# Block means kept in the value buffers, one token to a partition for keys and queries, PSUM banks given out singly, a shorter weight conversion, and a new plan

## The chip, the cores and the metric

The kernel runs on one core of a Trainium2 chip. The metric is the device time of one execution in microseconds (us). A core has five engines that this text names: TensorE (PE, matrix products; its weight loads are shown apart as PEld), VectorE (DVE), ScalarE (ACT), GpSimd (POOL) and SyncE (SP, which here only issues DMAs). They run their own instruction queues in order and wait for one another through semaphores. PE writes its results into eight PSUM banks.

## The reference

Three layers run one after the other on 1536 tokens (2 batches of 768): attention with 8 heads of 64, a gated layer, and a layer with an ELU. The weights arrive as 64-bit floats, q, k and v as 32-bit floats.

```python
# attention: block = 32, window = 16
k_sum = k.reshape(B, H, nb, block, D).max(axis=3)      # 24 block maxima of the keys
v_sum = v.reshape(B, H, nb, block, D).mean(axis=3)     # 24 block means of the values
scores_l = scale * q @ k^T, kept where |i - j| < 16
scores_s = scale * q @ k_sum^T + log(block)
a = softmax(concat(scores_l, scores_s))
x = a @ concat(v, v_sum)
# gated layer
xn = x / sqrt(mean(x * x) + 1e-6) * rms_g
x = (silu(xn @ w_gate) * (xn @ w_val)) @ w_out          # 512 -> 1536 -> 512
# ELU layer
h = x @ w_in                                            # 512 -> 2048
out = where(h > 0, h, exp(min(h, 0)) - 1) @ w_out2      # -> 512
```

## The kernel before

**Attention** goes in 24 tiles of 64 queries (12 for each batch), all heads at once. A tile needs 96 local keys and values (its own 64 and 16 on each side) and the 24 block maxima and means: 120 columns. The steps of a tile: `copy_keys` (POOL or ACT) builds the key tile `ka` from the transposed keys `kT` and the maxima `ksum`; for the first 8 tiles `premask` puts the mask into PSUM by matmuls; `scores` adds the products, so that mask and scores stand in one bank; `row_max` (DVE), `exps` (ACT), `guard` and `invert` (DVE), `normalize` (POOL for the first 8 tiles, else ACT), `turn_e` (PE transposes), `copy_e` (out of PSUM), `apply_v` (PE), `copy_x`. Since the maxima reach over all 768 keys of a batch, no scores can start until all its keys have been loaded, transposed, copied and reduced.

**Keys, queries, values.** A key load `load_k` brings 256 tokens of four heads, two neighbouring tokens to a partition, so that a run in memory is 512 bytes; the transposes then yield two half tiles that two copies interleave into `kT`. The first 512 queries come in the same way (`load_qq`, `turn_qq`, `copy_qq`), later ones one token to a partition (`load_q`, 256-byte runs). `mean_v` computes the block means by matmuls into PSUM; `copy_v` takes them to SBUF, four DMAs (`place_v`) bring them to a tile `vs`, and one more DMA for each attention tile (`load_vs`) copies `vs` into rows 96 to 119 of that tile's value buffer `va`, of which there are four.

**Weights** pass a chunk of 512 KB at a time through four staging buffers: `fetch` (SP), then the conversion from the 64-bit words: `convert_a` scales the high words as 32-bit floats (ACT), `convert_b` shifts them by three bits and clears the sign bit, `convert_c` puts the sign back, `convert_d` adds the low bits (all DVE). `split_a` and `split_b` turn a chunk into a coarse and a fine part, and three matmuls with these parts stand for one precise product (`project`, `down`).

**Order.** Tokens go through the gated layer in three blocks of 512, then through the ELU layer. A planner, `Order`, holds every step with its engine, a cost in us and a due time, simulates the engines and issues the steps in the order in which they start there; `pool` tags are buffers that a step takes, and a step waits in the plan for a free one. The table `SHIFT` moves due times by the step's name and the stretch of the run. PSUM: two banks under the tag `mm`, two under `at`, and `a0` to `a3`, one each; the tables `EARLY`, `KTAGS`, `QTAGS` and `VTAG` say by hand which tag a step of the first eight tiles takes.

Of the kernel before, what the change touches and what calls it, by code (L numbers as in the profile page):

```python
# [21 lines left out]
P = 128  # L22
BLOCK = 32
# [11 lines left out]
LIGHT = {"mean_v": 0.7, "apply_v": 0.65, "turn_qq": 0.5}  # L35


class Order:
# [34 lines left out]
    def issue(self):  # L73
# [47 lines left out]

        def can(i):
            need = {}
            for tag, name in ops[i][7]:
                need[tag] = need.get(tag, 0) + 1
                if self.slots[tag][1] and name not in queue[tag][:need[tag]]:
                    return False
            return all(free[tag] >= k for tag, k in need.items())
# [4 lines left out]
        while len(started) < n or events:  # L133
            for engine in list(soon):
# [18 lines left out]
                for tag, name in new:  # L153
# [37 lines left out]
def fused_kernel(ctx: ExitStack, tc: tile.TileContext, q, k, v, w_gate, w_val, w_out, rms_g, w_in2, w_out2, out):  # L191
# [45 lines left out]
    pool("va", 4, True)  # L237
# [4 lines left out]
    pool("vs", 1, True)  # L242
# [7 lines left out]
    for tag, bufs in (("mm", 2), ("at", 2), ("a0", 1), ("a1", 1), ("a2", 1), ("a3", 1)):  # L250
        pool(tag, bufs, space=PSUM)
# [34 lines left out]
    ANY_2 = {DVE: 0.6}, {POOL: 1.22, DVE: 0.6}, {POOL: 1.22}  # L286
# [101 lines left out]
    def convert_a(eng, kind, c):  # L388
        hi = words(kind, c).bitcast(F32)
        times(eng, hi, hi, 2.0 ** -112)  # L390

    def convert_b(kind, c):
        hi = words(kind, c)
        t = new("raw", f"raw_{kind}{c}", [P, 512], U32)
        nc.vector.tensor_scalar(
            t, hi, 3, 0x7FFFFFF8, op0=ALU.logical_shift_left, op1=ALU.bitwise_and)
# [74 lines left out]
    def add_k(b, due, gap, tags):  # L471
        add("-", 0.0, due, take, "ksum", f"ksum{b}", [P, NP, NB], w=[f"ksum{b}"], new=[("ksum", f"ksum{b}")])
        for i in range(NG):
            j, g = divmod(i, 2)
            tag = tags[i % len(tags)]
            n = f"{b}_{j}{g}"
            at = due + gap * i
            add("SP", 0.73, at - 4, load_k, b, j, g, w=[f"kr{n}"], new=[("raw", f"kr{n}")])
            add(PE, 0.44, at, turn_k, b, j, g, tag, r=[f"kr{n}"], w=[f"kt{n}"], new=[(tag, f"kt{n}")])
            if g == 0:  # L480
                add("-", 0.0, at - 1, take, "kT", f"kT{b}_{j}", [P, NP, 2 * P], w=[f"kT{b}_{j}"], new=[("kT", f"kT{b}_{j}")])
            for r in range(2):
                add(ANY if b == 0 else {ACT: 0.48}, 0, at + 0.5, copy_k, b, j, g, r,
                    r=[f"kt{n}", f"kT{b}_{j}"] + [f"kT{b}_{j}#{g}0"] * r, w=[f"kT{b}_{j}#{g}{r}"])
            if g:
                add(DVE, 1.15, at + 1, max_k, b, j, r=[f"kT{b}_{j}#{gg}{r}" for gg in range(2) for r in range(2)] + [f"ksum{b}"],
                    w=[f"ksum{b}#{j}"])

    def add_q(b, j, due, tag):
        rq, pt, qb = f"qr{b}_{j}", f"qt{b}_{j}", f"qbd{(b * NG + j) % 2}"  # L490
        add("SP", 1.46, due - 6, load_q, b, j, w=[rq], new=[("t2", rq)])
        add(PE, 0.44, due, turn_q, b, j, tag, r=[rq], w=[pt], new=[(tag, pt)])
        for h in range(2):
            add({ACT: 0.48}, 0, due + 0.5, copy_q, b, j, h, r=[pt], w=[f"{qb}#{h}{r}" for r in range(2)])


    def load_qq(j, g):
        nc.sync.dma_start(
            out=new("t2", f"qq{j}{g}", [P, NP, 2, D]),
            in_=q[0].rearrange("(a g) s d -> g a s d", g=2)[g, :, j * 2 * P:(j + 1) * 2 * P, :].rearrange(  # L500
                "h (p r) d -> p h r d", r=2))

    def turn_qq(j, n, tag):
        pt = new(tag, f"qt0_{2 * j + n}", [P, 2, NP, 64])
        ps = slice(64 * n, 64 * n + 64)
        for g in range(2):
            for pr in range(NP):
                nc.tensor.transpose(
                    pt[:, g, pr, :], T[f"qq{j}{g}"][ps, pr].rearrange("p r d -> p (r d)"), ident[ps, ps])

    def copy_qq(eng, j, g, r):
        src = T[f"qt0_{j}"][64 * r:64 * r + 64, g].rearrange("p a (t c) -> p t a c", t=2)
        dst = qbd[j % 2][64 * g:64 * g + 64, :, :, g].rearrange("p t a (c r) -> p t a c r", r=2)[:, :, :, :, r]
        times(eng, dst, src, scale)

    def add_qq(m, due, load, tag):
        j, n = divmod(m, 2)
        if n == 0:
            for g in range(2):
                add("SP", 0.73, load + 0.1 * g, load_qq, j, g, w=[f"qq{j}{g}"], new=[("t2", f"qq{j}{g}")])  # L520
        pt, qb = f"qt0_{m}", f"qbd{m % 2}"
        add(PE, 0.5, due, turn_qq, j, n, tag, r=[f"qq{j}0", f"qq{j}1"], w=[pt, f"{qb}#00"], new=[(tag, pt)])
        for g in range(2):
            for r in range(2):

                add({ACT: 0.27, DVE: 0.33}, 0, due + 0.5, copy_qq, m, g, r,
                    r=[pt] + [f"{qb}#{g}0"] * r + [f"{qb}#0{r}"] * g, w=[f"{qb}#{g}{r}"])
# [530 lines left out]
```

## Time and profile before

| what | us |
|---|---|
| median of 3 runs (lowest, highest) | 654.74 (654.32, 657.03) |
| the profiled execution | 653.92 |
| its span, first to last instruction | 652.2 |
| PE busy in it | 639.4 (98%) |
| DVE, ACT, POOL busy | 477.2, 374.5, 68.7 |

The profile is one execution; its span is 1.7 us shorter than the time that was measured for it, what lies before its first and behind its last instruction. Busy time is the union of the instructions' durations on an engine. PE's matmuls overlap, so that the distance from one start to the next says more about their price than their length: 12 matmuls of 512 columns take 2.72 us in a full stretch.

### The profile page before, as it was taken

The page shows a single profiled execution, that of the slowest core. Times are in us where ns is not written, and L with a number is a line of the kernel's source. Part 1 is how long each engine was busy: PE and PEld are TensorE (multiplying, and loading weights), DVE is VectorE, ACT ScalarE, POOL GpSimd, SP SyncE. Part 2 cuts the span into 40 slices and gives each one's busy share as a digit, 9 for nine tenths or more (in the row PEclk, how much of TensorE's full clock was granted, in tenths as well). Part 3 has the DMA queues.
Part 4 walks back from the last instruction along what each step waited for, and adds up shares of the span by engine and source line. Part 5 has one row for each costly group of instructions (what it writes and reads, how often), then busy time and mean ns, then how long its engine had stood idle before and what let it go on. Part 6 is the DMA issues. An engine that isn't in the chain of part 4 may idle for free.

```text
span 652.2 us, 9445 instructions
## 1 busy us (share of the span) xinstructions
PE 639.4 (98%) x3440; PEld 528.4 (81%) x3440; DVE 477.2 (73%) x860; ACT 374.5 (57%) x829; POOL 68.7 (11%) x125
## 2 busy tenths in 40 slices
PE   7899999999999999999999999999999999999997
PEld 5788787888888888888888888888888888888886
DVE  6899998998945545599999996555675555755554
ACT  5887888878856655655555555443454444544441
POOL 4731103125200100300000000000000000000000
PEclk9999999999999999999999999999999999999999
DMA  9785995653120400003655520000010000100001
GB/s 255 196 236 163 268 282 162 200 168 88 33 47 3 140 1 2 0 13 119 205 180 163 162 65 1 0 1 1 1 65 0 2 0 1 53 13 2 0 1 64
DMA packets 69917, 54.70 MB, mean 84 GB/s; under 512 B 29168, under 2 KB 64176, under 8 KB 69872
## 3 DMA queue, kind: packets, MB, share of 16 engines
q1 hardware_dynamic: 69872, 54.11, 28.8%
q8 instruction: 27, 0.44, 0.3%
q14 instruction: 18, 0.15, 0.1%
HBM read 49.68 MB, written 3.15 MB: 81 GB/s over the span
## 4 chain that ended last, share of the span: by engine, by line
PE 91%; DVE 3%; DMA 2%; ACT 2%; SPq 1%; issue 1%; POOL 0%; ACTq 0%; POOLq 0%
PE acc L893 35%; PE ph L825 20%; PE pg L825 14%; PE s L617 3%; PE pv L667 2%; PE pv_7c L825 1%; PE pv_9c L825 1%; PE pv_11c L825 1%; PE pv_1c L825 1%; DMA va<-vs 1%; PE pv_10c L825 1%; PE pv_6c L825 1%; PE pv_5c L825 1%; PE pv_8c L825 1%; PE pv_2c L825 1%; PE pv_3c L825 1%
## 5 line engine op out<-in xcount | busy, mean ns | idle before, releaser
L825 PE MATMUL ph<-xb,ws_i 128*128 128x512 f32 x576 | 137.9, 389 | 0.0
L893 PE MATMUL acc<-ws_p,act 128*128 128x512 f32 x576 | 137.7, 389 | 0.0
L825 PEld LDWEIGHTS ph<-xb,ws_i 128*128 128x128 f32 x576 | 108.1, 188 | 22.5
L893 PEld LDWEIGHTS acc<-ws_p,act 128*128 128x128 f32 x576 | 108.1, 188 | 22.4
L893 PE MATMUL acc<-act,ws_o 128*128 128x512 f32 x432 | 106.4, 393 | 0.0
L825 PE MATMUL pg<-x,ws_g 128*128 128x512 f32 (+1 forms) x432 | 106.3, 390 | 0.0
L893 PEld LDWEIGHTS acc<-act,ws_o 128*128 128x128 f32 x432 | 80.2, 188 | 16.6
L825 PEld LDWEIGHTS pg<-x,ws_g 128*128 128x128 f32 x432 | 78.2, 188 | 15.3 <-issue 0.2
L283 DVE TENSOR_TENSOR ws_p<-raw_p,ws_p 128x512 fp32r<-128x512 f32 x48 | 33.1, 690 | 48.8 <-ACT ws_p L272 48.8
L272 ACT CAST ws_p<-raw_p 128x512 fp32r<-128x512 f32 x48 | 29.8, 621 | 63.1 <-PE ph L825 57.3
L272 ACT CAST act<-ex 128x512 fp32r<-128x512 f32 x48 | 29.8, 622 | 55.9 <-DVE ex L873 39.3
L880 DVE TENSOR_TENSOR act<-ex,act 128x512 fp32r<-128x512 f32 x48 | 33.1, 691 | 31.3 <-ACT act L272 30.9
L283 DVE TENSOR_TENSOR ws_i<-raw_i,ws_i 128x512 fp32r<-128x512 f32 x48 | 33.1, 689 | 19.1 <-ACT ws_i L272 19.0
L272 ACT CAST ws_i<-raw_i 128x512 fp32r<-128x512 f32 x48 | 29.7, 619 | 28.5 <-PE ph L825 23.1
L283 DVE TENSOR_TENSOR ws_g<-raw_g,ws_g 128x512 fp32r<-128x512 f32 x35 | 25.6, 732 | 18.4 <-ACT ws_g L272 18.0
L272 ACT CAST ws_o<-raw_o 128x512 fp32r<-128x512 f32 x36 | 22.4, 621 | 26.3 <-PE acc L893 6.3
L272 ACT CAST ws_g<-raw_g 128x512 fp32r<-128x512 f32 x35 | 21.6, 618 | 24.9 <-PE pg L825 13.2
L873 DVE SCALAR_TENSOR_TENSOR ex<-ph,ex 128x512 f32<-128x512 f32 x48 | 33.2, 691 | 1.5
L272 ACT CAST ws_v<-raw_v 128x512 fp32r<-128x512 f32 x35 | 21.7, 619 | 16.7 <-PE pv_1c L825 3.2
L283 DVE TENSOR_TENSOR ws_v<-raw_v,ws_v 128x512 fp32r<-128x512 f32 x35 | 25.0, 714 | 6.0 <-ACT ws_v L272 5.9
L272 ACT CAST act<-th 128x512 fp32r<-128x512 f32 x36 | 22.3, 618 | 11.6 <-PE acc L893 5.8
L865 ACT ACTIVATE ex<-ph 128x512 f32<-128x512 f32 x48 | 28.5, 593 | 0.0
(209 smaller groups left out, 987.6 us busy)
## 6 DMA issues: line engine op xcount, KB each, us to landing
st_i<-in_moe_w_in SPq DMA_DIRECT2D x16, 512.0 KB
st_p<-in_moe_w_out SPq DMA_DIRECT2D x16, 512.0 KB
st_g<-in_moe_w_gate SPq DMA_DIRECT2D x12, 512.0 KB
st_v<-in_moe_w_val SPq DMA_DIRECT2D x12, 512.0 KB
st_o<-in_moe_w_out SPq DMA_DIRECT2D x12, 512.0 KB
va<-in_v SPq DMA_DIRECT2D x20, 192.0 KB
kr<-in_k SPq DMA_DIRECT2D x12, 256.0 KB
vtok<-in_v SPq DMA_DIRECT2D x6, 512.0 KB
```

What stands on the lines that cost most here:

```text
L272: nc.scalar.copy(out=out, in_=in_)
L283: (nc.gpsimd if eng == POOL else nc.vector).tensor_sub(out, a, b)
L617: nc.tensor.matmul(pq[:, pr, :], qb[:, t % 2, pr].rearrange("p h c -> p (h c)"), ka[:, pr, :], start=not pre, stop=not pre or pr == NP - 1)
L667: nc.tensor.matmul(pv[64 * h:64 * h + 64, pr, :], va[:, 2 * pr + h, :], at[:, pr, QT * h:QT * h + QT], start=True, stop=True)
L825: nc.tensor.matmul(pt[:, i], wt[:, a, kk * P:(kk + 1) * P], xt[:, c, kk, i], start=(kk == 0 and n == 0), stop=(kk == KM - 1 and n == 2))
L865: nc.scalar.activation(out=new("t2", f"ex{b}_{c}", [P, TB]), in_=T[f"ph{b}_{c}"], func=AF.Exp)
L873: nc.vector.scalar_tensor_tensor(ex, T[f"ph{b}_{c}"], 0.0, ex, op0=ALU.max, op1=ALU.add)
L880: nc.vector.tensor_sub(t[:, 1], T[src], t[:, 0].bitcast(F32))
L893: nc.tensor.matmul(acc, lhsT, rhs, start=(first and n == 0), stop=(last and n == 2))
```

## The change

- The block means stay where they are needed: there are four fixed value buffers `va_bufs` that the tiles use in turn. For the first batch four copies (DVE or ACT) bring the means from PSUM into rows 96 to 119 of buffer 0, for the second batch from the SBUF copy `vm`; `repeat_v` (POOL or ACT) copies them to the other three. `load_vs`, the tile `vs` and its DMAs are gone; a tile loads its 96 values alone.
- Keys and all queries are loaded one token to a partition, in 256-byte runs; a key load covers 128 tokens of all heads, one copy takes its transposes to `kT`, and the maxima are taken by 128 tokens.
- Each PSUM bank has a tag of its own, and a step may name several tags: `pick` takes the first that is free. A new tag `pm` lets at most three mask preloads be open, and a preload waits in the plan for the batch's last maximum.
- For the chunks of `w_gate`, `w_val` and `w_out` (`SIGNED`), the scaling on ACT becomes a parametric ReLU, whose slope for negative values, -2^32, leaves them positive with one exponent bit more, and the shift by three moves that bit into the sign's place. `convert_c` isn't issued for them. `w_in` and `w_out2` keep it.
- Costs, due times and the table `SHIFT` are new (56 entries before, 384 now, of which two stand below).

```diff
@@ Order: a step may name several tags
+        def pick(i):
+            need, found = {}, []
+            for tags, name in ops[i][7]:
+                for tag in tags if isinstance(tags, tuple) else (tags,):
+                    n = need.get(tag, 0) + 1
+                    if free[tag] >= n and (not self.slots[tag][1] or name in queue[tag][:n]):
+                        break
+                else:
+                    return None
+                need[tag] = n
+                found.append((tag, name))
+            return found
...
@@ banks and value buffers
-    for tag, bufs in (("mm", 2), ("at", 2), ("a0", 1), ("a1", 1), ("a2", 1), ("a3", 1)):
-        pool(tag, bufs, space=PSUM)
+    MM, AT, ACC = ("m0", "m1"), ("t0", "t1"), ("a0", "a1", "a2", "a3")
+    BANKS = AT + MM + ACC[::-1]
+    for tag in BANKS:
+        pool(tag, 1, space=PSUM)
+    o.pool("pm", PM)
+    va_bufs = [const.tile([P, H, D], F32, name=f"va{i}") for i in range(VA)]
...
@@ conversion
-        times(eng, hi, hi, 2.0 ** -112)
+        if kind in SIGNED:
+            nc.scalar.activation(out=hi, in_=hi, func=AF.Prelu, scale=2.0 ** -112, alpha=-2.0 ** 32)
+        else:
+            times(eng, hi, hi, 2.0 ** -112)
...
+        if kind in SIGNED:
+            nc.vector.tensor_scalar(t, hi, 3, None, op0=ALU.logical_shift_left)
...
-        add(DVE, 0.6, need - 6.5, convert_c, kind, c, r=[st, raw], w=[raw])
+        if kind not in SIGNED:
+            add(DVE, 0.6, need - 6.5, convert_c, kind, c, r=[st, raw], w=[raw])
...
@@ keys
-    def load_k(b, j, g):
+    def load_k(b, i):
         nc.sync.dma_start(
-            out=new("raw", f"kr{b}_{j}{g}", [P, NP, 2, D]),
-            in_=k[b].rearrange("(a g) s d -> g a s d", g=2)[g, :, j * 2 * P:(j + 1) * 2 * P, :].rearrange(
-                "h (p r) d -> p h r d", r=2))
+            out=new("raw", f"kr{b}_{i}", [P, H, D]),
+            in_=k[b, :, i * P:(i + 1) * P, :].rearrange("h p d -> p h d"))
...
+    def copy_k(eng, b, i):
+        j, r = divmod(i, 2)
+        copy(eng, T[f"kT{b}_{j}"][:, :, r * P:(r + 1) * P], T[f"kt{b}_{i}"])
...
@@ block means
-    def place_v(b):
+    def place_v(eng, b):
+        src = T[f"vm{b}"] if b else T[f"vp{b}"]
         for g in range(4):
-            nc.sync.dma_start(out=T[f"vs{b}"][:, 2 * g:2 * g + 2], in_=T[f"vm{b}"][32 * g:32 * g + NB])
+            copy(eng, va_bufs[0][NL:NK, 2 * g:2 * g + 2], src[32 * g:32 * g + NB])
+
+    def repeat_v(eng, i):
+        if eng == POOL:
+            nc.gpsimd.tensor_scalar(va_bufs[i][NL:NK], va_bufs[0][NL:NK], 1.0, 0.0, op0=ALU.mult, op1=ALU.add)
+        else:
+            copy(eng, va_bufs[i][NL:NK], va_bufs[0][NL:NK])
...
+    def add_place(b, due, gap):
+        add({ACT: 0.72, DVE: 0.6} if b == 0 else {POOL: 1.0}, 0, due, place_v, b, r=[f"vm{b}" if b else f"vp{b}"], w=["va0#s"])
+        for i in range(1, VA):
+            add({POOL: 0.6, ACT: 0.52} if b == 0 else {POOL: 0.6}, 0, due + gap * i, repeat_v, i, r=["va0#s"], w=[f"va{i}#s"])
...
-    def load_vs(b, t):
-        nc.sync.dma_start(out=T[f"va{b}_{t}"][NL:NK], in_=T[f"vs{b}"])
...
@@ tiles
-            add(PE, 0.32, due - 1.5, premask, b, t, tags[1], r=[f"mask_b{mask_of(t)}"], w=[f"s{n}"], new=[(tags[1], f"s{n}")])
+            add(PE, 0.32, due - 1.5, premask, b, t, tags, r=[f"mask_b{mask_of(t)}", f"ksum0#{NG - 1}"],
+                w=[f"s{n}", f"pm{n}"], new=[(tags, f"s{n}"), ("pm", f"pm{n}")])
...
@@ plan
-LOOK, URGENT = 0.2, 20
-A0, A_GAP, LATER = 12.1, 1.275, -1.0
+SIGNED = 'gvo'
+LOOK, URGENT = -0.3, 5
+A0, A_GAP, LATER = 11.8, 1.775, 0.0
...
-TILE8, GAP_1, GAP_2 = 8.0, 10.0, 12.5
+TILE8, GAP_1, GAP_2 = 3.0, 9.4, 10.2
...
+K0, QL, VA, PM = 2.1, (1.4, 5.0, 9.5, 11.5), 4, 3
...
+    ('act_a', 0): -6, ('act_b', 0): -2.5, ('add_mask', 0): 3, ('add_square', 0): 10, ('apply_v', 0): -16.5,
...
-LEN_A, LEN_1, LEN_2 = 8.675, 7.55, 5.35
+LEN_A, LEN_1, LEN_2 = 8.575, 7.55, 6.15
```

How the instructions stand on three engines, before and now. In the names `kr`, `qr` and `qq` are loaded keys and queries, `kt` and `qt` their transposes, `vtok` values for the block means, `vp` the means in PSUM, `s` scores, `at` transposed probabilities, `st_g` a staged weight chunk; a number behind a name counts the tile.

SP's queue from the last key load on, a few rows skipped, before:

```order
L445 DMA kr_21_177<-in_k 128x4x128
L498 DMA qq_218<-in_q 128x4x128
L498 DMA qq_220<-in_q 128x4x128
L530 DMA vtok_0_228<-in_v 128x8x128 x2
L530 DMA vtok_1_229<-in_v 128x8x128
L577 DMA va_0_263<-in_v 80x8x64
L498 DMA qq_329<-in_q 128x4x128
L498 DMA qq_332<-in_q 128x4x128
L577 DMA va_1_278<-in_v 96x8x64
L549 DMA vs_405<-vm_412 24x128 x4
L580 DMA va_0_263<-vs_405 24x512
L580 DMA va_1_278<-vs_405 24x512
```

And now, the same stretch:

```order
L466 DMA kr_5_183<-in_k 128x8x64
L454 DMA qr_0_185<-in_q 128x8x64
L454 DMA qr_1_205<-in_q 128x8x64
L515 DMA vtok_0_229<-in_v 128x8x128 x2
L515 DMA vtok_1_230<-in_v 128x8x128
L454 DMA qr_2_274<-in_q 128x8x64
L575 DMA va_136<-in_v 80x8x64
L454 DMA qr_3_291<-in_q 128x8x64
L575 DMA va_137<-in_v 96x8x64
L575 DMA va_138<-in_v 96x8x64
L575 DMA va_139<-in_v 96x8x64
L395 DMA st_g_462<-in_moe_w_gate 128x4x128
```

The query loads come in singly, two ahead of the values for the means and two between the values of the first tiles; the DMAs of the means (`vs` and `va` from `vs`) are gone.

PE from the last transposes ahead of the first scores on, before (the mask preloads of tiles 4, 5, 6, 1 and 0 stand ahead of these rows):

```order
L609 MATMUL s_2_335<-log_lo,ident_b 128x4x24
L539 MATMUL vp_342<-vtok_0_228,blocks 32x128 x16
L617 MATMUL s_0_314<-ka_0_361,qbd_133 128x120 x4
L617 MATMUL s_1_309<-ka_1_367,qbd_133 128x120 x4
L539 MATMUL vp_342<-vtok_1_229,blocks 32x128 x8
L617 MATMUL s_2_335<-ka_2_381,qbd_134 128x120 x4
L508 MATMUL qt_2_434<-ident,qq_329 128x64 x4
L656 MATMUL at_0_456<-ident,e_0_370 120x128 x4
L617 MATMUL s_3_414<-ka_3_399,qbd_134 128x120 x4
L508 MATMUL qt_3_475<-ident,qq_329 128x64 x4
```

And now, where the first row follows the transposes of the last keys (of a preload only its first matmul is shown):

```order
L462 MATMUL qt_0_293<-ident,qr_0_185 128x128 x4
L602 MATMUL s_0_306<-mask_b_166,ident_b 128x480
L462 MATMUL qt_1_310<-ident,qr_1_205 128x128 x4
L602 MATMUL s_1_318<-mask_b_167,ident_b 128x480
L613 MATMUL s_0_306<-ka_0_302,qbd_140 128x120 x4
L613 MATMUL s_1_318<-ka_1_315,qbd_140 128x120 x4
L524 MATMUL vp_340<-vtok_0_229,blocks 32x128 x8
L602 MATMUL s_2_360<-mask_b_167,ident_b 128x480
L613 MATMUL s_2_360<-ka_2_335,qbd_141 128x120 x4
L524 MATMUL vp_340<-vtok_1_230,blocks 32x128 x8
L652 MATMUL at_0_419<-ident,e_0_324 120x128 x4
```

The first scores now stand behind the transposes of the second query load; four mask preloads and the steps of the block means that stood ahead of them stand behind them, and so does the first transpose of probabilities, as before.

DVE between the first key copy and the first query copy, before (the cast of a mask between them isn't shown):

```order
L274 COPY kT_0_176<-kt_00_196 64x512 x2
L274 COPY kT_1_195<-kt_10_248 64x512
L461 TENSOR_REDUCE ksum_179<-kT_0_176 128x4x8
L274 COPY kT_2_217<-kt_21_273 64x512
L274 COPY kT_2_217<-kt_20_267 64x512
L461 TENSOR_REDUCE ksum_179<-kT_1_195 128x4x8
L461 TENSOR_REDUCE ksum_179<-kT_2_217 128x4x8
```

And now:

```order
L290 COPY kT_0_187<-kt_0_221 128x4x128
L483 TENSOR_REDUCE ksum_203<-kT_0_187 128x4x4 x2
L483 TENSOR_REDUCE ksum_203<-kT_1_204 128x4x4 x2
L483 TENSOR_REDUCE ksum_203<-kT_2_228 128x4x4 x2
L296 TENSOR_SCALAR qbd_140<-qt_0_293 64x8x64
L296 TENSOR_SCALAR qbd_141<-qt_1_310 64x8x64
```

DVE copies one key tile where it copied five half ones (ACT has the other copies), and takes six smaller maxima instead of three.

## Rows read from the trace of the kernel before

**Rows 1.** Windows: stretch; its us, busy per engine (instructions), PEclk, DMA share, GB/s
```profile
0.00:15.00 15.00, 10.29 (x96) 7.68 (x97) 9.99 (x21) 8.28 (x15) 7.20 (x37) 1.00 0.95 256
15.00:41.00 26.00, 23.07 (x284) 20.14 (x285) 21.95 (x55) 21.14 (x85) 16.78 (x30) 1.00 0.90 228
41.00:60.00 19.00, 18.73 (x130) 17.04 (x127) 18.44 (x42) 14.26 (x34) 5.61 (x9) 1.00 0.62 172
60.00:100.00 40.00, 39.02 (x273) 31.07 (x271) 36.53 (x66) 32.99 (x84) 6.11 (x7) 1.00 0.91 249
100.00:300.00 200.00, 200.00 (x1135) 164.39 (x1134) 148.33 (x266) 135.28 (x331) 33.00 (x44) 1.00 0.25 73
300.00:648.00 348.00, 348.00 (x1537) 288.05 (x1535) 241.29 (x413) 162.57 (x284) 0.00 (x0) 1.00 0.15 47
```

**Rows 2.** Timeline of PE, 8 to 45: start, us, instructions [idle before <-releaser]
```profile
10.23 0.70 PE L508 MATMUL qt<-ident,qq 64*128 64x64 f32 x8
10.87 0.38 PE L606 MATMUL s<-mask_b,ident_b 128*128 128x480 bf16 x1
...
11.16 0.37 PE L606 MATMUL s<-mask_b,ident_b 128*128 128x480 bf16 x1
...
14.27 2.05 PE L617 MATMUL s<-ka,qbd 128*128 128x120 f32 x16
16.24 0.65 PE L539 MATMUL vp<-vtok,blocks 128*32 128x128 f32 x16
16.82 1.15 PE L617 MATMUL s<-ka,qbd 128*128 128x120 f32 x8
...
20.04 0.65 PE L656 MATMUL at<-ident,e 128*120 128x128 f32 x4 [1.03 <-POOL e L648]
...
36.93 0.66 PE L439 MATMUL qt<-ident,qr 128*128 128x128 f32 x4
37.42 0.64 PE L656 MATMUL at<-ident,e 128*120 128x128 f32 x4
...
41.22 1.99 PE L836 MATMUL pg<-xT,raw_g 128*128 128x256 f32 x8
```

**Rows 3.** Windows of 2 us with different loads, columns as in rows 1
```profile
2.00:4.00 2.00, 0.07 (x1) 0.10 (x2) 1.70 (x8) 0.06 (x1) 1.67 (x11) 1.00 0.90 268
...
8.00:10.00 2.00, 1.85 (x16) 1.37 (x16) 1.58 (x2) 1.93 (x4) 0.04 (x1) 1.00 1.12 335
18.00:20.00 2.00, 1.01 (x11) 0.74 (x9) 1.67 (x5) 2.00 (x14) 1.86 (x4) 1.00 1.12 181
34.00:36.00 2.00, 2.00 (x20) 2.00 (x19) 2.00 (x6) 2.00 (x5) 0.00 (x0) 1.00 1.22 298
```

**Rows 4.** Timeline of PE's weight loads, the last keys' transposes
```profile
8.78 0.42 PEld L454 LDWEIGHTS kt<-ident,kr 128*128 128x128 f32 x4 [0.35 <-ACT kT L272]
```

**Rows 5.** Timeline of DVE, 8 to 15: last key copies and maxima
```profile
9.47 1.41 DVE L274 COPY kT<-kt 64x512 f32<-64x512 f32 x2 [0.42 <-PE kt L454]
10.80 2.33 DVE L461 TENSOR_REDUCE ksum<-kT 128x32 f32<-128x1024 f32 x2
```

**Rows 6.** Timeline of POOL, 12 to 15: maxima into the first key tile
```profile
13.22 0.28 POOL L585 TENSOR_SCALAR ka<-ksum 128x96 f32<-128x96 f32 x1 [5.17 <-DVE ksum L461]
```

**Rows 7.** Chain of waits, 25 to 50: start, us, what
```profile
27.58 5.07 DMA va<-vs
...
34.66 3.25 DMA va<-vs
...
39.61 0.57 DVE raw_g L400
...
45.30 0.60 DVE raw_v L400
```

**Rows 8.** Groups by shape, 0 to 250: line, tiles, count | busy us, mean ns | idle
```profile
L278 ACT ACTIVATE st_g<-st_g 128x512 f32<-128x512 f32 x12 | 8.2, 685 | 0.4 <-DMA st_g<-in_moe_w_gate 0.4
...
L400 DVE SCALAR_TENSOR_TENSOR raw_g<-st_g,raw_g 128x512 uint32<-128x512 uint32 x12 | 8.2, 686 | 0.0
```

More of the change, by code (lines that the diff above doesn't have):

```diff
@@ L120, in issue @@
                 offer(i)
-        def can(i):
[L123 to L128, printed above, removed]
+        def pick(i):
[10 more added lines that the diff above has]
+            return found
+        def can(i):
+            return pick(i) is not None
         def shared(i, engine):
@@ L152, in issue @@
                     soon[e].remove(best)
-                for tag, name in new:
+                for tag, name in pick(best):
+                    home[name] = self.tag_of[name] = tag
                     free[tag] -= 1
@@ L285, in fused_kernel @@
     ANY = {ACT: 0.48, DVE: 0.6}
-    ANY_2 = {DVE: 0.6}, {POOL: 1.22, DVE: 0.6}, {POOL: 1.22}
+    ANY_2 = {DVE: 0.6}, {POOL: 1.28, DVE: 0.6}, {POOL: 1.28}
     ANY_SB = {ACT: 0.52}
@@ L481, in add_k @@
                 add("-", 0.0, at - 1, take, "kT", f"kT{b}_{j}", [P, NP, 2 * P], w=[f"kT{b}_{j}"], new=[("kT", f"kT{b}_{j}")])
[L482 to L487, printed above, removed]
@@ L489, in add_q @@
-    def add_q(b, j, due, tag):
+            add(ANY if b == 0 else {ACT: 0.48}, 0, at + 0.5, copy_k, b, i, r=[f"kt{n}", f"kT{b}_{j}"], w=[f"kT{b}_{j}#{r}"])
+            add(DVE, 0.6, at + 1, max_k, b, i, r=[f"kT{b}_{j}#{r}", f"ksum{b}"], w=[f"ksum{b}#{i}"])
+    def add_q(b, j, load, due, tag):
         rq, pt, qb = f"qr{b}_{j}", f"qt{b}_{j}", f"qbd{(b * NG + j) % 2}"
-        add("SP", 1.46, due - 6, load_q, b, j, w=[rq], new=[("t2", rq)])
+        add("SP", 1.0, load, load_q, b, j, w=[rq], new=[("t2", rq)])
@@ L492, in add_q @@
         add(PE, 0.44, due, turn_q, b, j, tag, r=[rq], w=[pt], new=[(tag, pt)])
         for h in range(2):
[L494 to L527, printed above, removed]
+            add(ANY if b * NG + j < TPB // 2 else {ACT: 0.48}, 0, due + 0.5, copy_q, b, j, h, r=[pt], w=[f"{qb}#{h}"])
@@ L788, in add_norm @@
             if n >= n_sums:
-                add(POOL, 1.22, due + 0.6 * n, add_square, blk, cs, i, r=[sq], w=[first])
+                add(POOL, 1.28, due + 0.6 * n, add_square, blk, cs, i, r=[sq], w=[first])
         y = f"{blk}{i}"
@@ L896, in add_down @@
         for i, ms in enumerate(groups):
-            add(PE, 0.648 * len(ms), due + 1.3 * i, down, names, ms, act, ws, first, last, feature_major,
+            add(PE, 0.68 * len(ms), due + 1.36 * i, down, names, ms, act, ws, first, last, feature_major,
                 r=[act + "#h", act + "#l", ws + "#h", ws + "#l"], w=[names[m] for m in ms],
@@ new lines @@
+    ('load_q', 2): -8, ('load_v', 2): 2, ('mean_square', 2): -9.5, ('normalize', 2): 4.5, ('place_v', 2): -9,
+    ('premask', 2): 1.5, ('project', 2): -2, ('project_f32', 2): 4.5, ('repeat_v', 2): -4, ('root', 2): -24,
+    ('row_max', 2): -8, ('scale_x', 2): 7, ('scores', 2): -1, ('split_a', 2): -3, ('spread', 2): 4,
+    ('square', 2): 1, ('store', 2): 0.5, ('sum_square', 2): -8.5, ('take', 2): 8, ('turn_e', 2): 0.5,
+    ('turn_k', 2): -8, ('turn_q', 2): 1, ('x_lo', 2): 1.5, ('zero_v', 2): -8, ('act_a', 3): 2,
```

220 lines of the change are left out of this document (138 added, 82 removed), and 4 rows, old and new, of the table EARLY.

## Prediction

> **What bounds the kernel now.** I read the stages first [rows 1]: six stretches, each with TensorE's (PE's) busy time beside its length. From 100 to 648 us PE is busy 548.00 of 548 us, at a granted clock of 1.00 throughout. Nothing done for the other engines there can shorten the run, unless PE itself gets less to do. PE is idle 4.71 us before 15 us, 2.93 from 15 to 41, 0.27 from 41 to 60, 0.98 from 60 to 100, and the last 4 us are the output's copy and store, which the change leaves as they are. So the change is worth what it does to about 9 us of idle time, plus what it does to PE's own work, plus a little that busy time hides.
>
> Next I read PE's own order in the attention of the first 512 tokens [rows 2]. A step's price on PE is the distance from its start to the next one's: a mask preload 0.29 us (10.87 to 11.16), eight query transposes 0.64 (10.23 to 10.87), four transposes of 128 tokens 0.49 (36.93 to 37.42), a block-mean step of 16 matmuls 0.58 (16.24 to 16.82), one tile's scores 0.98 (two in 14.27 to 16.24). The first scores start at 14.27 and the first projection at 41.22. Who keeps PE waiting before 14.27 is the key path: the last key load lets its transposes start at 8.78 [rows 4], VectorE (DVE) copies until 10.88 and takes maxima until 13.13 [rows 5], GpSimd (POOL) writes the maxima into the key tile from 13.22 [rows 6]. Later, the chain of waits [rows 7] runs through two DMAs that bring the block means into a value buffer (5.07 and 3.25 us from issue to landing), then through DVE's conversion of weights.
>
> **The start: keys and queries one token to a partition.** The six key loads and the first two query loads keep their bytes (1.57 and 0.52 MB), but fall from 512-byte to 256-byte pieces, so twice as many. The stretches of 512-byte pieces ran at 268 GB/s (the keys themselves) and 335 [rows 3]; the value rows, which are 256-byte pieces in this kernel too, ran at 181 GB/s from 18 to 20 us, and 298 from 34 to 36, with weights among them. I take 240, the middle. The keys then need 1.57/0.240 = 6.5 us where they needed 1.57/0.268 = 5.9: +0.7, with ends -0.6 (at 298) and +2.8 (at 181).
>
> The Trainium skill speaks against this part: "DMA: Bandwidth & Descriptors", section "Why small descriptors are slow (HBM only)", has a fixed overhead of three cycles on each packet, 11 cycles for the eight beats of 256 bytes. By that 512 bytes take 19 cycles and two of 256 take 22, so the keys would need 16% longer, an estimate of +0.9 us instead of +0.7. The rows at 181 and 298 GB/s lie on both sides of it.
>
> What follows the keys gets shorter. Each load now needs one whole copy instead of two half ones, and one maximum over 512 elements instead of 1024 for two loads (1.21 us in rows 5, half is 0.60). After the last load: transposes 0.49, copy 0.65, maximum 0.60, POOL 0.28, four handovers of 0.1: 2.4 us, where 8.78 to 13.5 was 4.7. Key tile ready: 8.78 + 0.7 + 2.4 = 11.9. But the first scores now stand behind the second query load on PE (the order shows it): 0.52 MB at 240 GB/s is 2.2 us, so 8.78 + 0.7 + 2.2, then transposes 0.49 and a mask preload 0.29: **12.5**, against 14.27, a gain of 1.8 (ends: 10.7 and 15.3). Against that, PE does less ahead of them: four mask preloads (at most three are now open) and two block-mean steps move behind, 4 x 0.29 + 2 x 0.58 = 2.3 us. The idle time of the start grows by **+0.5** (ends -1.2 and +3.3).
>
> **From the first scores to the first projection.** The eight copies and 24 loads of block means disappear, and with them the two DMA waits of rows 7. In their place come four DVE copies out of PSUM, three repeats on POOL and ScalarE (ACT), all of at most 24 x 512 elements, and no wait on SyncE (SP). The four value buffers were four before, so a load of values still waits for the tile four back. What is late next: the first transposes of probabilities, which waited 1.03 us for POOL at 20.04 [rows 2]. On POOL the key tile of tile 4 is ahead of that normalization and itself waits for the scores of tile 2. By steps: scores 3 x 0.98, block means 0.58, preload 0.29, then 0.95 of POOL copies and 1.0 of normalization give 5.8 us after the first scores; PE has 3 x (0.98 + 0.58 + 0.29) = 5.5 to do until then. So 0.3 of wait remain here. I leave 1.0 of the 2.93 idle for the stage, the 0.3 and twice as much again for the other in-order waits: **-1.9** (ends -2.9 and 0; ACT was busy 21.14 and DVE 21.95 of 26 us [rows 1], so there is little slack). The query transposes of four tile pairs cost 4 x 0.49 instead of 4 x 0.64 on PE: **-0.6**, sure, since it is work.
>
> **The sign step.** 36 weight chunks lose one DVE operation of 0.69 us [rows 8], 25 us, of which 20 or so fall before 100 us. The scaling on ACT stays one instruction and becomes another function; its own cost isn't shown, the nearest row is the scaling at 0.69 us, and I take that (as cheap as a cast, 0.62, or as dear as two passes, 1.4). At 36 of them the dear end is +25 us on an engine that is busy 33 of 40 us from 60 to 100, so it could stop PE for a few us there. The order has a single table load for ACT in both kernels, so no reload is added. DVE's relief is worth only what PE waits for: two of these operations lie on the chain, 0.57 and 0.60 us [rows 7], around the norm of the first block, and 0.98 us of PE's idle time lies from 60 to 100, with DVE busy 36.53 of 40. I take **-1.0** (ends -1.3 and +2). From 100 to 300 us PE shows no idle time, and the late operands hide under modelled ends; I take **-0.5** (ends -2 and +1). From 300 us on: 0.
>
> **Smaller edits.** PSUM banks given out singly and the new due times only reorder; what they do is in the terms above. In the second batch the block means are planned on POOL, but the copy helper sends everything that isn't ACT to DVE: four small copies, below 0.3 us each, at about 90 us, hidden under a full PE; uncovered they would cost 1.1.
>
> **Sum.** +0.5 - 1.9 - 0.6 - 1.0 - 0.5 = -3.5 us. The profiled execution took 653.92 us: 653.92 - 3.5 = **650.4**. The median of the runs, 654.74, is 0.8 above it, so the gain against the median reads as 4.3 us or 0.7%.
>
> **Rivals.**
> *More.* With DVE 25 us lighter and no DMA in the value path, all 4.18 us of idle from 15 to 100 go, the start gets its good end (-1.2), queries -0.6, and the 100 to 300 stretch -1: 646.9. For it: the chain's waits there are nearly all on the removed work. Against it: ACT at 21.14 of 26 us gets no lighter.
> *Given back.* PE reaches the first projection earlier, but the weights for it aren't there: DVE was busy 18.44 of 19 us from 41 to 60, and the value loads and weights share one queue. Then only the queries' 0.6 and a few tenths remain: 653.0. Against it: that DVE time shrinks by a fifth.
> *Slower: the small pieces.* Place: the eight loads ahead of the first scores. At 181 GB/s these start at 15.3, and with 2.3 us of work moved behind them the start loses 3.3; if the stages behind then keep their idle time as before, only the 0.6 is regained: 656.6. Eight such loads at once may run below the slowest stretch that the trace has, so 658 and more is open. By itself it decides from the point where the start costs 4.0 us, what the other terms gain: first scores at 16.0, that is the eight loads below some 170 GB/s. For it: 181 was measured with the queue busy 1.12. Against it: 298 at 1.22.
> *The change doesn't do what it says:* the placing that runs on another engine than planned is the one such place, priced above.
>
> **How the numbers follow.** Forecast 0.50 (own range 648.0 to 652.5), more 0.20, given back 0.15, slower 0.15. The range 645.5 to 656.5 leaves out about 0.07 above and 0.08 below. A measurement can tell 0.5%, 3.3 us: faster is below 651.5, slower above 658.0. Faster: 0.38 of the forecast and 0.20 of "more", 0.58. Slower: two thirds of the slower rival, 0.10. Same: 0.32.
>
> **What would show it.** In the profile after: no DMA into value buffers but from the values; first scores between 10.7 and 15.3, mean rate of the first 8 us near 240 GB/s; first projection about 40 to 41; the ACT scaling of gate chunks near 0.69 us; PE's idle time from 15 to 100 us near 2 us; PE full from 100 us on. It is wrong if the first scores come after 15.5, if the new scaling takes over 1 us, or if PE shows idle time behind 100 us.

## The result and the profile after

The changed kernel takes **660.46 us** (median of 4 runs, 660.16 to 660.50); the kernel before took 654.99 beside it. The ratio is 1.0079, with a 95% interval of 1.0059 to 1.0098: slower by 0.8%, where 0.7% faster was forecast, and outside the range of 645.5 to 656.5. The profiled execution has a span of 658.0 us against 652.2.

The stages of the changed kernel, columns as in [rows 1]:

```profile
0.00:15.00 15.00, 8.71 (x54) 6.45 (x54) 9.46 (x22) 5.40 (x8) 7.69 (x38) 1.00 1.04 218
15.00:41.00 26.00, 25.36 (x327) 21.81 (x326) 19.81 (x54) 22.73 (x87) 19.05 (x37) 1.00 1.06 250
41.00:60.00 19.00, 18.30 (x120) 16.70 (x119) 18.35 (x45) 15.47 (x43) 4.12 (x4) 1.00 0.59 171
60.00:100.00 40.00, 39.90 (x295) 32.30 (x294) 31.20 (x57) 30.55 (x74) 8.96 (x12) 1.00 1.06 278
100.00:300.00 200.00, 197.58 (x1099) 161.68 (x1098) 134.80 (x253) 127.26 (x317) 30.59 (x42) 1.00 0.21 62
300.00:648.00 348.00, 348.00 (x1512) 281.25 (x1511) 237.83 (x411) 158.86 (x278) 0.00 (x0) 1.00 0.14 45
```

PE's idle time, the length less its busy time, is 6.29, 0.64, 0.70, 0.10 and 2.42 us in the first five stretches, against 4.71, 2.93, 0.27, 0.98 and 0. In the sixth no idle time shows in either kernel, but PE starts 1512 matmuls there, not 1537. All are of the long kind at 0.227 us (2.72 for 12), so 25 fewer are 5.7 us that a busy share of 100% hides.

| stretch | forecast | measured |
|---|---|---|
| 0 to 41 us, idle | +0.5 - 1.9 = -1.4 | 6.93 - 7.64 = -0.7 |
| 41 to 100, idle | -1.0 | 0.80 - 1.25 = -0.45 |
| query transposes | -0.6 | -0.6 (distances to the next start without the waits in them: 5.42 against 6.07 in all) |
| 100 to 300, idle | -0.5 | +2.4 |
| behind 300 | 0 | +5.7 |
| sum | -3.5 | +6.35; PE's last start is 6.13 later |

So the first 100 us went the forecast's way at about half its size, and the loss lies behind 100 us. PE's timeline, as in [rows 2], has the first scores 1.03 us and the first projection 1.09 us earlier than before:

```profile
13.24 2.01 PE L613 MATMUL s<-ka,qbd 128*128 128x120 f32 x16
...
40.13 1.90 PE L831 MATMUL pg<-xT,raw_g 128*128 128x256 f32 x8
```

In the chain of waits, which ran through two DMAs of block means [rows 7], the only DMA before 45 us is now the last key load; the means are short DVE copies:

```profile
5.12 4.95 DMA kr<-in_k
...
19.08 0.28 DVE va L290
```

**Around 100 us.** The timeline of all engines shows the only long wait of PE behind 15 us (the next one is 0.67). `place_v` of the second batch runs on DVE (L290); then GpSimd repeats the means (L541) while DVE shifts and converts two chunks; the guard of the first tile's sums (L635) stands behind them, ACT's normalization (L647) waits for it and for the reciprocal, and PE's transposes wait 1.66 us:

```profile
100.53 0.93 DVE L290 COPY va<-vm 24x128 f32<-24x128 f32 x4
...
101.61 2.58 POOL L541 TENSOR_SCALAR va<-va 24x512 f32<-24x512 f32 x3 [1.58 <-DVE va L290]
...
101.83 0.85 DVE L415 TENSOR_SCALAR raw_v<-st_v 128x512 uint32<-128x512 uint32 x1
...
102.61 1.14 DVE L428 SCALAR_TENSOR_TENSOR raw_g<-st_g,raw_g 128x512 uint16<-128x512 uint16 x1
...
103.64 1.15 DVE L428 SCALAR_TENSOR_TENSOR raw_v<-st_v,raw_v 128x512 uint16<-128x512 uint16 x1
...
104.68 0.42 DVE L635 TENSOR_SCALAR ss<-ss 128x4 f32<-128x4 f32 x1
...
105.41 1.25 ACT L647 ACTIVATE e<-e,rs 128x120 f32<-128x120 f32 x4 [2.26 <-DVE rs L639]
...
106.60 0.62 PE L652 MATMUL at<-ident,e 128*120 128x128 f32 x4 [1.66 <-DVE e L618]
```

The bracket at 106.60 names DVE L618, which only happens to end last; what the transposes read is ACT's result, and the delay comes from the instructions ahead of the guard in DVE's queue.

**The ELU layer.** One step in the timeline: DVE's last reading of a product `ph` ends at 511.35, the weight load for the next `ph` starts 0.12 us later, having stood 0.32, and 12 matmuls take 2.98 us:

```profile
510.66 0.69 DVE L868 SCALAR_TENSOR_TENSOR ex<-ph,ex 128x512 f32<-128x512 f32 x1
...
511.47 2.59 PEld L820 LDWEIGHTS ph<-xb,ws_i 128*128 128x128 f32 x12 [0.32 <-issue]
511.50 2.98 PE L820 MATMUL ph<-xb,ws_i 128*128 128x512 f32 x12
```

By groups from 300 us on, these products have a mean of 394 ns, where those of the kernel before have 389, and their weight loads show 9.0 us of idle time ended by "issue", which those of the second product (`acc`) don't show:

```profile
L820 PE MATMUL ph<-xb,ws_i 128*128 128x512 f32 x576 | 141.7, 394 | 0.0
...
L820 PEld LDWEIGHTS ph<-xb,ws_i 128*128 128x128 f32 x576 | 105.9, 188 | 30.3 <-issue 9.0
```

Two lines of the diff that the prediction did not quote stand behind it. The bank of `ph` alternated between two tags of two banks each; now the plan takes the first bank that it holds free:

```diff
-            add_project(f"ph{n}", ("mm", "at")[c % 2], f"ws{b}_i{c}", x, [0], t)
+            add_project(f"ph{n}", MM + AT, f"ws{b}_i{c}", x, [0], t)
```

The plan gives out `m0` again and again: in 30 of 47 steps the bank is that of the step before. It counts the bank as free when the simulated reader ends; in the trace the reader ends later, and the weight load stands for it. All 28 slow steps of the trace are among these 30: the starts on both sides of their first matmul lie 0.315 and 0.306 us apart in place of 0.227, and in all a step takes 0.20 us more (two such products start 5.63 us apart at 511.50 and 517.13; 5.44 where the bank changes, at 384.68 and 390.12). For the 28 steps that is the whole 5.7.

### The profile page after: what moved, and what is told of

It is laid out like the page before. It is cut to its first block, busy times and chain, and to the rows that moved or that the text cites. A ratio compares the mean times of both kernels' runs of the same rounds, so it can differ in the third digit from the quotient of the medians.

```text
span 658.0 us, 9324 instructions
## 1 busy us (share of the span) xinstructions
PE 644.2 (98%) x3424; PEld 525.1 (80%) x3424; DVE 455.3 (69%) x842; ACT 360.9 (55%) x805; POOL 70.4 (11%) x130
## 4 chain that ended last, share of the span: by engine, by line
PE 90%; DVE 4%; ACT 3%; POOL 1%; DMA 1%; SPq 1%; issue 1%; ACTq 0%; POOLq 0%
PE acc L888 34%; PE ph L820 21%; PE pg L820 14%; PE s L613 2%; PE pv L663 2%; PE pv_3c L820 1%; PE pv_7c L820 1%; PE pv_8c L820 1%; PE pv_2c L820 1%; PE pv_11c L820 1%; PE pv_6c L820 1%; PE pv_9c L820 1%; PE at L652 1%; PE pv_1c L820 1%; PE pv_10c L820 1%; PE pv_4c L820 1%
## 5 line engine op out<-in xcount | busy, mean ns | idle before, releaser
L820 PE MATMUL ph<-xb,ws_i 128*128 128x512 f32 x576 | 141.7, 394 | 0.0
L820 PEld LDWEIGHTS ph<-xb,ws_i 128*128 128x128 f32 x576 | 105.9, 188 | 30.3 <-issue 9.0
L299 DVE TENSOR_TENSOR ws_p<-raw_p,ws_p 128x512 fp32r<-128x512 f32 x48 | 33.2, 691 | 74.1 <-ACT ws_p L288 74.1
L299 DVE TENSOR_TENSOR ws_g<-raw_g,ws_g 128x512 fp32r<-128x512 f32 x35 | 24.6, 704 | 19.0 <-ACT ws_g L288 18.9
L299 DVE TENSOR_TENSOR ws_i<-raw_i,ws_i 128x512 fp32r<-128x512 f32 x48 | 32.9, 685 | 6.9 <-ACT ws_i L288 6.9
L853 DVE SCALAR_TENSOR_TENSOR th<-th,pg 128x512 f32<-128x512 f32 x36 | 24.6, 684 | 6.6 <-ACT th L849 6.4
L875 DVE TENSOR_TENSOR act<-th,act 128x512 fp32r<-128x512 f32 x36 | 25.1, 696 | 4.7 <-ACT act L288 4.4
```

The lines of the kernel that those rows point to most:

```text
L299: (nc.gpsimd if eng == POOL else nc.vector).tensor_sub(out, a, b)
L820: nc.tensor.matmul(pt[:, i], wt[:, a, kk * P:(kk + 1) * P], xt[:, c, kk, i], start=(kk == 0 and n == 0), stop=(kk == KM - 1 and n == 2))
L853: nc.vector.scalar_tensor_tensor(th, th, 1.0, T[f"pg{b}_{c}"], op0=ALU.add, op1=ALU.mult)
L875: nc.vector.tensor_sub(t[:, 1], T[src], t[:, 0].bitcast(F32))
```

## The experiments

Ratios are to the kernel before, run beside each, with 95% intervals.

**Banks of the last layer in turn (e1_alt).**

```diff
-            add_project(f"ph{n}", MM + AT, ...
+            add_project(f"ph{n}", ("m0", "t0")[c % 2], ...
```

> Only the bank of the last layer's products is changed: m0 and t0 in turn, where the plan gave m0 to 30 of 47 steps that follow a step in m0. The order on every engine stays. Theory A (a step in the bank of the one before waits until VectorE has read that one): the steps at 315 and 306 ns go back to 227, PE's lost time behind 400 us falls from 5.1 to about 0, and the time falls by 5.5 us, from 660.5 to about 655.0. Rival B (the new order or the new due times of the last layer cost it, whichever bank is used): the long steps stay and the time stays at 660.5.

Measured: 656.18 us, ratio 1.0021 (1.0012 to 1.0030): 4.3 us less than the changed kernel. Theory A holds: the 28 slow steps are gone. Two stops are left: a matmul that takes 0.55 us more than 0.227, and the next one 0.08 more. They lie where three products follow each other at the change of the token block, so that with two banks the third meets the first:

```profile
474.06 0.69 DVE L868 SCALAR_TENSOR_TENSOR ex<-ph,ex 128x512 f32<-128x512 f32 x1
...
474.86 2.12 PEld L820 LDWEIGHTS ph<-xb,ws_i 128*128 128x128 f32 x10 [0.78 <-issue]
474.89 2.29 PE L820 MATMUL ph<-xb,ws_i 128*128 128x512 f32 x9 [0.39 <-DVE ex L868]
```

Expected were 5.5; the two stops are 1.3 of the 1.2 that is missing.

**The second batch's means off DVE (e2_pool), and left out (e2_none).**

```diff
-            copy(eng, va_bufs[0][NL:NK, 2 * g:2 * g + 2], src[32 * g:32 * g + NB])
+            if eng == POOL:
+                nc.gpsimd.tensor_copy(va_bufs[0][NL:NK, 2 * g:2 * g + 2], src[32 * g:32 * g + NB])
+            else:
+                copy(eng, va_bufs[0][NL:NK, 2 * g:2 * g + 2], src[32 * g:32 * g + NB])
...
@@ e2_none instead: place_v and repeat_v, second batch
+        if b:
+            return
```

> The four copies of the second batch's block means go to GpSimd, as planned, and no longer to VectorE; all else stays. Theory A (these copies, 0.93 us on VectorE at 100.5 us, stand ahead of the conversions and the guard on which the first normalization of the second batch waits, and PE waits 1.66 us for that at 106.6): PE's wait falls to about 0.7 and the time by 0.9 us, to 659.5. Rival B (the conversions would have been late anyway, slowed beside GpSimd's repeats): the wait stays near 1.7 and the time at 660.5.

> The second batch's block means are left out behind PSUM (no copies into the first value buffer, no repeats on GpSimd), so that its output lacks them; the order of all else stays. Theory A (copies and the 2.58 us of repeats beside VectorE's conversions are the whole of the wait at 106.6): that wait goes, 1.7 us, and the time is 658.7. If only the copies count: 659.5. Rival B (the order of the conversions alone makes the normalization late): 660.5.

Measured: 658.33, ratio 1.0050 (1.0036 to 1.0065), and 658.29, 1.0051 (1.0036 to 1.0065): 2.1 and 2.2 us less, and the same. PE's wait is gone in both. In the timeline of e2_pool the conversions run beside GpSimd's copies and take 0.86 us:

```profile
101.00 2.32 POOL L538 COPY va<-vm 24x128 f32<-24x128 f32 x4 [0.52 <-ACT vm L532]
...
101.63 0.86 DVE L428 SCALAR_TENSOR_TENSOR raw_g<-st_g,raw_g 128x512 uint16<-128x512 uint16 x1
102.34 0.86 DVE L428 SCALAR_TENSOR_TENSOR raw_v<-st_v,raw_v 128x512 uint16<-128x512 uint16 x1
...
105.22 0.60 PE L655 MATMUL at<-ident,e 128*120 128x128 f32 x4
```

and in e2_none, with GpSimd free, 0.76 (and the shift before them 0.42):

```profile
101.18 0.42 DVE L415 TENSOR_SCALAR raw_v<-st_v 128x512 uint32<-128x512 uint32 x1
...
101.52 0.76 DVE L428 SCALAR_TENSOR_TENSOR raw_g<-st_g,raw_g 128x512 uint16<-128x512 uint16 x1
102.15 0.76 DVE L428 SCALAR_TENSOR_TENSOR raw_v<-st_v,raw_v 128x512 uint16<-128x512 uint16 x1
...
105.18 0.60 PE L656 MATMUL at<-ident,e 128*120 128x128 f32 x4
```

So both parts counted: 0.93 us of copies, and beside the repeats that the copies released 0.8 of slower conversions and 0.4 of a slower shift (0.85 against 0.42). Theory A of e2_pool was right in the place and had less than half of the size, since it left the second part where it was. Only that wait is tested by this: PE's other idle time from 100 to 300 us (0.41 us before scores at 150 that wait for ACT's query copy, some smaller ones, 0.76 in all) stays in e2_pool and e2_none, isn't there in the kernel before, and wasn't tried.

**Both edits (e3_both), and four banks in turn (e8_four).**

```diff
-            add_project(f"ph{n}", MM + AT, ...
+            add_project(f"ph{n}", ("m0", "t0", "m1", "t1")[c % 4], ...
```

> Alternating banks in the last layer together with the copies on GpSimd. If the two add up, by the theories of the single runs: 660.5 - 5.5 - 0.9 = 654.1. If the time won at 106 us is lost again to a later wait for VectorE: 655.0, as with the banks alone.

> As the kernel with both edits, but the last layer's products go through four banks in turn, not two; the order on every engine stays. With two banks PE stood twice for 0.55 and 0.08 us (matmuls of 778 and 306 ns, at 473 and 561 us), where at the change of the token block three products follow each other closely. Theory A (a bank still being read): both stops go, 1.26 us, and 654.75 becomes 653.5. Rival B (the conversion of the weights is late at the change of the block): the stops stay, 654.7.

Measured: 654.75, ratio 0.9999 (0.9990 to 1.0008); with four banks **653.32, ratio 0.9964 (0.9951 to 0.9978)**, faster than both kernels. The products' mean and idle times of weight loads, by groups of e8_four from 300 us on, are back at 389 ns and no wait:

```profile
L823 PE MATMUL ph<-xb,ws_i 128*128 128x512 f32 x576 | 138.5, 389 | 0.0
...
L823 PEld LDWEIGHTS ph<-xb,ws_i 128*128 128x128 f32 x576 | 108.1, 188 | 22.4
```

For e8_four theory A holds. e3_both lies between its two cases: the copies on GpSimd are worth 1.4 us here, 2.1 alone. By windows PE's idle time from 100 to 300 us falls from 2.47 in e1_alt to 0.75, so no later wait there takes the gain back; what the other 0.7 us are stays open. The banks and the place of four copies turn 0.8% slower into 0.4% faster.

**The sign step alone, in the kernel before (b4_sign), and put back in the changed one (e4_sign).** In both the order stays:

```diff
@@ b4_sign: kernel before, with the new scaling and shift
     def convert_c(kind, c):
+        if kind in SIGNED:
+            return
...
@@ e4_sign: changed kernel, alternating banks, old scaling and mask
     def convert_d(kind, c):
+        if kind in SIGNED:
+            convert_c(kind, c)
```

> The kernel before with the short conversion alone: the parametric ReLU for the chunks of w_gate, w_val and w_out, and no sign step for them; order and due times as before. Theory A (VectorE's load costs PE in the first 100 us, the forecast's term of -1.0 and -0.5 behind 100): 653.5. Rival B (PE's waits there hang on the DMAs of the block means and on the order, not on VectorE's load): 655.0.

> The changed kernel with two alternating banks in the last layer (656.2), and the sign step put back for all chunks, in the place where the last step of the conversion stands; 36 operations of 0.69 us more on VectorE, the order otherwise unchanged. Theory A (the new plan needs the relief): PE waits for weights again, at least the 1.5 us of the forecast's two terms, 657.7 or more. Rival B (VectorE has room): 656.2.

Measured: b4_sign 653.57, ratio 0.9981 (0.9967 to 0.9996), some 1.2 us less, as theory A had it. e4_sign 680.51, ratio 1.0377 (1.0358 to 1.0396), 24 us more than e1_alt. The direction is A's, the size was not expected: it is about that of the DVE work put back, 36 operations of 0.69 us, which doesn't yet show that it is the same time. Its windows show PE idle 6 and 8 us, and a granted clock below 1.00, so that part of the stretch ran at 1.2 GHz:

```profile
60.00:100.00 40.00, 34.03 (x202) 26.81 (x202) 35.08 (x60) 27.25 (x68) 4.86 (x4) 0.96 0.83 216
100.00:150.00 50.00, 41.92 (x262) 32.29 (x262) 44.46 (x76) 28.26 (x67) 12.12 (x16) 0.94 0.63 178
```

The old order gains 1.2 us by the relief; the new one loses 24 without it.

**Small pieces, in the kernel before (e5_pieces).** Each key load and load of the first queries becomes two DMAs with pieces of 256 bytes:

```diff
+        for r in range(2):
+            nc.sync.dma_start(out=t[:, :, r], in_=src[:, :, r])
```

> The kernel before with each key load and each load of the first queries as two DMAs of 256-byte pieces; bytes, destinations and all else stay. Theory A (small pieces lower the rate, 268 GB/s to the 222 that the changed kernel shows in its first 10 us): the last keys come 1.3 us later, the first scores start at 15.6 and the time is 656.3. Rival B (the later start is hidden, since PE has preloads and block means to do, and the wait for the values' DMA shrinks by as much): 655.0.

Measured: 659.85, ratio 1.0064 (1.0049 to 1.0079), 4.2 us more. Theory A has the cause and a third of the price. Windows of e5_pieces, first its loads, then PE's stop and what follows:

```profile
2.00:4.00 2.00, 0.09 (x1) 0.12 (x2) 1.70 (x8) 0.06 (x1) 1.67 (x11) 1.00 0.96 217
...
8.00:10.00 2.00, 1.89 (x9) 1.15 (x8) 1.43 (x2) 1.23 (x3) 0.23 (x1) 1.00 1.21 230
```
```profile
33.00:36.00 3.00, 1.99 (x39) 1.59 (x37) 2.12 (x8) 3.00 (x14) 2.56 (x5) 1.00 1.03 206
36.00:38.00 2.00, 1.47 (x19) 1.39 (x20) 0.88 (x3) 2.00 (x10) 0.68 (x1) 0.70 1.17 302
38.00:41.00 3.00, 3.00 (x20) 3.00 (x19) 2.54 (x6) 1.81 (x4) 0.95 (x1) 0.63 0.88 196
```

The loads ran at 217 and 230 GB/s in windows where [rows 3] has 268 and 335. The weight load of the last keys' transposes starts at 9.93, 1.15 us later than in [rows 4], near the 1.3 of theory A, but the first scores at 16.44, 2.2 us later: PE's own steps were slower there too (a mask preload took 0.60 us at 10.84, 0.37 in [rows 2]). PE then stands 1.0 us of 3 from 33 on (from 15 to 41 its idle time is 3.97, 1.0 more than before), and the clock granted from 36 to 41 is 0.70 and 0.63, so that PE ran part of it at 1.2 GHz in place of 2.4: 0.30 of 2 us and 0.37 of 3 are up to 1.7 us lost. The 2.2, 1.0 and 1.7 us make 4.9 of the 5.0 by which the first projection comes later in the profile (46.26 against 41.22); this one execution is 5.9 us longer than the profiled one of the kernel before, more than the 4.2 of the medians.

What in the pieces is slow stays open, the transfer or the issue: from one of these DMAs to the next SyncE took 0.55 us, and 131 KB every 0.55 us are 238 GB/s.

**Means by DMA (e6_dma8).** From e8_four; in the first batch `repeat_v` becomes

```diff
+            nc.sync.dma_start(out=va_bufs[i][NL:NK], in_=va_bufs[0][NL:NK])
```

> The kernel with both edits and four banks (653.3, PE idle 0.65 us from 15 to 41 us), but the first batch's block means go from value buffer 0 to the other three by DMAs on SyncE's queue, as copies into value buffers did before, not by GpSimd and ScalarE. Theory A (such DMAs, 3.25 and 5.07 us from issue to landing in the chain of the kernel before, made its waits before 41 us): the value products of tiles 1 to 3 wait, PE's idle time there rises by 1 to 2 us, 654.3 to 655.3. Rival B (the new order leaves these tiles so late that a DMA would have landed): 653.3.

Measured: 654.43, ratio 0.9997 (0.9987 to 1.0007), against 0.9964. PE's idle time from 15 to 41 us rises from 0.65 to 1.78:

```profile
15.00:41.00 26.00, 24.22 (x320) 20.75 (x320) 18.97 (x51) 20.00 (x80) 17.34 (x32) 1.00 1.01 230
```

The size is A's, its way is not: tiles 1 to 3 don't wait. The three issues hold SyncE for 2.4 us at 20.6, and the loads queued behind them are later: a chunk of `w_out` is issued at 29.76 in place of 27.63, ACT's scaling waits for it, ACT's copy of transposed probabilities behind that is late, and the value product at 38.73 us waits 1.25.

```profile
36.84 0.67 ACT L407 ACTIVATE st_o<-st_o 128x512 f32<-128x512 f32 x1 [1.24 <-DMA st_o<-in_moe_w_out]
```

**The plan (e10_oldplan, e4b_plan, b5_signplan).** From e8_four with the old numbers; from e8_four with `SIGNED = ''`; the kernel before with the short conversion known to its planner.

```diff
@@ e10_oldplan
-LOOK, URGENT = -0.3, 5
+LOOK, URGENT = 0.2, 20
... (with SHIFT and the spacings)
@@ e4b_plan
-SIGNED = 'gvo'
+SIGNED = ''
@@ b5_signplan
-        add(DVE, 0.6, need - 6.5, convert_c, kind, c, r=[st, raw], w=[raw])
+        if kind not in SIGNED:
+            add(DVE, 0.6, need - 6.5, convert_c, kind, c, r=[st, raw], w=[raw])
```

> The same kernel with the table of shifts, the look-ahead and the spacings of the kernel before; the steps and their costs stay. Theory A (the refit made the gain before 100 us and was needed): the first projection comes later than 40.1 and the time is 656 or more. Rival B (the planner's simulation orders the new steps as well by the old numbers, and the refit brought the waits behind 140 us): 653 or less.

> The same kernel with the sign step as before for all chunks, this time told to the planner, which simulates anew with the due times as they are. Put back without that it cost 24.3 us (680.5 against 656.2). Theory A (most of that came from an order made for less work on VectorE; the work itself is worth the forecast's 1.5 us): 654.8 to 657. Rival B (VectorE has no room, 25 us of work must come out somewhere in the first 150 us): 665 or more.

> The kernel before with the short conversion, this time told to its planner (without that it took 653.6). Theory A (the relief is used up by what PE waits for anyway): 653.6 again. Rival B (a plan that knows of the relief pulls more work ahead of the first projection): 652.5 or less.

Measured: 661.26, ratio 1.0101 (1.0085 to 1.0117); 658.71, 1.0055 (1.0041 to 1.0068); 659.85, 1.0078 (1.0065 to 1.0092). e10_oldplan is theory A: 9 us more than e8_four by the ratios, with the first projection late:

```profile
46.31 1.99 PE L834 MATMUL pg<-xT,raw_g 128*128 128x256 f32 x8
```

The other two give no price of the sign step. Taking work off DVE and telling the planner made the kernel before 6 us slower than taking it off untold (1.0078 against 0.9981), which is against both theories; adding work and telling the planner cost the new one 6 us, by the ratios. In all three runs a set of steps that was simulated with a table fitted to another set gave a worse order.

## Why the prediction was wrong

**The step that failed** is "PSUM banks given out singly and the new due times only reorder; what they do is in the terms above", with "From 300 us on: 0". That a step may now take any of several banks also decides which one it takes, and the first free one is the one just read. Measured: +5.7 us behind 300, of which two banks gave back 4.3 and four the rest. The full PE of [rows 1] was read as a stretch where nothing could be lost; it stays full only as long as a bank has been read before PE comes back to it. The Trainium skill states this in "Perfetto Trace Analysis", section "Matmuls": independent groups should rotate through the banks, so that one is emptied while the next is filled. The trace agrees, at 0.20 us for a step that comes back to the bank too early. That the cause is the bank, and not the new order or the due times, is shown: e1_alt beside the changed kernel and e8_four beside e3_both keep the order on every engine and differ in the bank alone.

**The term from 100 to 300 us** was -0.5 and came out +2.4, beyond its end of +1; idle time of PE behind 100 us was one of the prediction's own signs of being wrong. The rival that the placing runs on DVE was right on the fact and wrong on the price: "hidden under a full PE; uncovered they would cost 1.1". They cost 2.1 (e2_pool), being uncovered and, through the repeats that they let start, slowing a shift and two conversions besides. "At about 90 us" was 100.5, just where the new batch's first normalization needs DVE.

**The start** was priced at 240 GB/s and ran at 218 to 234; the first scores came at 13.24, not 12.5. The last keys' transposes start at 10.21, not 9.48, but the second query load is transposed at 11.79, close to the sum's 11.7; what the sum left out is the copy of the queries, for which PE waits:

```profile
12.96 0.36 PE L602 MATMUL s<-mask_b,ident_b 128*128 128x480 bf16 x1 [0.54 <-DVE qbd L296]
```

Nor was it the key path alone that kept PE until 14.27 in the kernel before. The key tile is ready at 13.50 [rows 6], and PE then still does a step of the block means that had waited for its load:

```profile
13.69 0.65 PE L539 MATMUL vp<-vtok,blocks 128*32 128x128 f32 x16 [0.30 <-DMA vtok<-in_v]
```

e5_pieces shows that the mechanism of the rival "small pieces" is real and costs the old kernel 4.2 us. In the new one the first scores are earlier all the same; which of its other edits there (one load for each step, earlier queries, the missing DMAs) makes up for it wasn't tried. The rival's sum, 656.6, came nearer to 660.46 than the forecast did by luck: its place was the start, and the loss lay behind 100 us. The prediction's estimate from the Trainium skill, "DMA: Bandwidth & Descriptors", section "Why small descriptors are slow (HBM only)", had the keys need 16% longer; 268 GB/s against the 222 from 4 to 6 us is 21%.

**Right** were the direct gains: the DMA waits of the means went (e6_dma8 brings back 1.1 us of idle time, by the queue), the scaling stays as cheap:

```profile
L407 ACT ACTIVATE st_g<-st_g 128x512 f32<-128x512 f32 x12 | 8.2, 685 | 2.9 <-DMA st_g<-in_moe_w_gate 2.9
```

and the sign step's -1.5 is within b4_sign's interval (-0.3 to -2.2), though its place isn't shown: in b4_sign's windows PE's idle time from 41 to 100 us falls from 1.25 to 0.74, and from 100 to 300 it was 0 and stays so. With the two faults mended, e8_four stands 2.4 us below the kernel before, by its ratio, where 3.5 were forecast.

## What to carry to other kernels

A pool of two buffers rotates; a search for the first free one does not. When a change replaces the one by the other, look for each repeated step at who reads its buffer last and whether that ends before the next write, also where the busy engine shows no idle time, and count instructions started in equal stretches rather than busy time. Mend such faults before judging a change, and don't price a step by a plan whose table was fitted to other steps.

## What the runs showed of the hardware

A DVE conversion with two operands (`convert_d`, 128x512) took 0.76 us with GpSimd free (e2_none), 0.86 beside its copies of 24x128 into a value buffer (e2_pool), and 1.14 beside its repeats of 24x512 from one value buffer to another (the changed kernel). The Trainium skill, "SBUF — State Buffer", section "Who interferes with whom", has it that a DVE instruction with two SBUF inputs contends with a GpSimd instruction that reads SBUF; for these conversions the trace agrees, and the price here, up to 0.38 us for each, was missing from the forecast. It isn't so for every pair: an add of two SBUF operands (L299, at 104.61 in e2_pool) took 0.68 us beside the same repeats, no more than elsewhere, while the shift of one operand took 0.85 in place of 0.42.

The issue of a load on SyncE went by pieces: six key loads of 512 pieces each took 3.29 us in the kernel before, six of 1024 took 5.48 in the changed one for the same bytes, and twelve of 512 took 6.48 in e5_pieces, about 1 ns a piece in all three. Timelines of SyncE, before and then after:

```profile
0.79 3.29 SPq L445 DMA_DIRECT2D kr<-in_k  x6
```
```profile
0.79 5.48 SPq L466 DMA_DIRECT2D kr<-in_k  x6
```
